# Joint last-key products, a tanh gate and a freer weight split in a capped-attention and gated-MLP kernel

## The chip, the cores and the metric

The kernel runs on one core of a Trainium2 chip. The metric is the device time of one execution in microseconds (us), as the median of several runs. The profile comes from one further execution, and its times are counted from the first instruction on the core.

## The reference

There are 4 batches, 12 heads, 448 positions and a head dimension of 64. Attention with capped scores feeds a gated MLP whose gate comes from a convolution over positions. Everything is float32 except the MLP weights, which are float64.

```python
scores = np.matmul(q, k.transpose(0, 1, 3, 2)) / np.sqrt(64)
scores = cap * np.tanh(scores / cap)
attn = np.exp(scores - max); attn = attn / (attn.sum(-1) + 1e-09)
x = np.matmul(attn, v)                     # heads joined: [4, 448, 768]
h = np.maximum(x @ w_in, 0.0)              # [4, 448, 1024]
conv_out = sum over 3 taps of conv_w[k] * h shifted by k-1 positions
gate = 1.0 / (1.0 + np.exp(-conv_out))
out = h * gate @ w_out                     # [4, 448, 768]
```

## The kernel before

**Attention.** The unit of work is a pair of heads of one batch: 24 pairs, 6 to a batch. Keys stand on the partitions and queries on the 448 free elements. A head has 448 keys, so a pair has three units `u = 0, 1, 2` of 128 keys per head (`NU = 3`) and a last unit `u = NU` with the remaining 64 keys of both heads, 128 rows in all. `scores` makes the score product of a unit into PSUM, then tanh and exp on ScalarE (L454, L458). A full unit is two products of 64 contraction rows by 128 keys, one per head, that sit in the two row halves of the array (planner mode `row`) and fill a two-bank tile `sp`. The last unit is one product of 128 by 128 (mode `full`), whose key block the host pads with zeros, into a one-bank tile `spr` from the pool `m` that the MLP uses too. Pairs 0 to 11 (`RAW`) multiply float32 directly; pairs 12 to 23 split q and k into a high and a low fp32r part (L402, L405, L256) and add three products. Two units of such pairs go into one task (`TWO = 12`).

`values` multiplies exp(scores) by V: four units, each two products of 128 by 64, one per head in a column half of the array (mode `col`), into the accumulator `acc`; the V block of the last unit is padded with zeros. All eight products of a pair are one task (`BUNDLE`).

**Key sums.** Pairs 0 to 3 (`normalize_early`) sum the keys by products with ones, eight of 128 by 32 per pair (mode `quad`). Later pairs first add the units on VectorE into `P` (L489), and the last unit by two additions on 64 partitions (L494, L497). Pairs 4 to 11 (`normalize`) sum `P` of two pairs by four products (L517) and take reciprocals of a small gathered copy that travels by DMA through DRAM (`cs`, `r_d`, `rb`). Pairs 12 to 23 (`normalize_one`, from `DIRECT = 12`) sum by two products of 128 by 64 (L631) and take the reciprocal of a whole 128x448 tile (L636). `split` then writes x as a high and a low part.

**MLP.** `feed_forward` runs 288 product steps of 128 by 128 by 448 per batch: 144 into `hps` (L674) and 144 into `ops` (L757). Between them ScalarE makes relu (L682) and the middle tap (L692), VectorE the outer taps (L700), ScalarE the sigmoid (L709) and VectorE the product with h (L715).

**Weights.** `weight_unit` turns float64 words into two fp32r parts: ScalarE scales the high word (L322), VectorE masks and shifts (L324, L326, L329), either engine makes the rounded part, VectorE the remainder. There are 12 units of 128x512 for w_in and 24 of 128x256 for w_out, which go back to DRAM (`wo`) and are loaded again in every batch.

**Order.** `Plan` orders all tasks of all engines at build time, and each engine then works through its list in that order. Of the tasks that can start, an engine's next is that of the earliest due time, from `STEP`, `FIRST` and `DUE`; TensorE adds `HOLD` for a change between `full` and a tiled mode and `CROSS` for one between tiled modes. `either` leaves the engine, ScalarE or VectorE, to the planner. All loads are issued on SP's queue. Pools bound what can be in flight: two `sp` tiles, two `acc` banks (key sums use them too), two `m` banks, 15 `e` buffers, two each for k and q.

Of the kernel before, what the change touches and what calls it, by code (L numbers as in the profile page):

```python
# [172 lines left out]
def capped_attention_gated_mlp_kernel(  # L173
# [17 lines left out]
    KW = KF + 128  # L191
# [71 lines left out]


# [42 lines left out]
    def weight_unit(src, n, due, stage, take, uses, deps, dst=None):  # L307
# [67 lines left out]
    prep, b_in, t_v, b_v = {}, {}, {}, {}  # L375
# [5 lines left out]
    def prepare(p):  # L381
# [5 lines left out]
        lk = dma("sp", 128 * KW * 4, lambda: new(p, raw_p, "kr", [128, KW]), lambda: k[b, j], ld, (), [bk],  # L387
# [3 lines left out]
        t_v[p] = dma("sp", 128 * KW * 4, lambda: new(p, raw_p, "vr", [128, KW], bufs=BUFS["v"]), lambda: v[b, j], ld + 3, (),  # L391
                     [b_v[p]], after=t0 - AHEAD["v"])
        if p in RAW:
            prep[p], b_in[p] = [lk, lq], [bq, bk]
            return
# [12 lines left out]
        def k_hi(eng):  # L408
            copy(eng, new(p, raw_p, "ks", [128, 2, KW], F32R, bufs=BUFS["s"])[:, 0], T[p]["kr"])

        def k_lo():
            sub(T[p]["ks"][:, 1], T[p]["kr"], f32(T[p]["ks"][:, 0]))
# [3 lines left out]
        c = either(KW, k_hi, due + 0.1, [lk, a], uses=[bk, bs])  # L416
        c2 = task("dve", dve(KW), k_lo, due + 0.4, [c], uses=[bk, bs])
        prep[p], b_in[p] = [a, a2, c, c2], [bs]

    def scores(units, due):  # L420

        rest = units[0][1] == NU
        n = 1 if rest else 2
        out = [{} for _ in units]
        bufs = [Buf("m" if rest else "sp") for _ in units]

        def qk():
            for (p, u), sp in zip(units, out):
                if rest:
                    sp[0] = ps_m.tile([128, 512], F32, tag="m", name="spr").rearrange("p (a s) -> p a s", a=1)  # L430
                else:
                    sp[0] = ps_s.tile([128, 2, 512], F32, tag="sp", name="sp")
                X = T[p]
                if p in RAW:
                    parts = [(X["kr"], X["qr"])]
                else:
                    parts = [(X["ks"][:, w], X["qs"][:, l]) for w, l in ((0, 0), (0, 1), (1, 0))]
                for i, (w, x) in enumerate(parts):
                    for h in range(n):
                        r = slice(0, 128) if rest else half[h]  # L440
                        nc.tensor.matmul(out=sp[0][:, h, 0:S], lhsT=w[r, 128 * u:128 * u + 128], rhs=x[r],  # L441
                                         start=i == 0, stop=i == len(parts) - 1)

        cost = sum(2 * HALF if p in RAW else 3 * PASS for p, u in units)
        t_qk = task("pe", cost, qk, due, [t for p, u in units for t in prep[p]], bufs,
                    [b for p, u in units for b in b_in[p]], mode="full" if rest else "row")
        for (p, u), sp, bsp in zip(units, out, bufs):
            t_u = when(p, u / (NU + 1))
            raw = p in RAW
            b_e[p, u] = Buf("e")  # L450

            def tanh(sp=sp, raw=raw):
                x = sp[0][:, 0:n, 0:S]
                nc.scalar.activation(out=x, in_=x, func=ACTF.Tanh, **({"scale": tsc_sb[:, 0:1]} if raw else {}))  # L454

            def exp(p=p, u=u, sp=sp):
                E[p, u] = e_p.tile([128, 2, S], F32, tag="e", name="E")
                nc.scalar.activation(out=E[p, u][:, 0:n], in_=sp[0][:, 0:n, 0:S], func=ACTF.Exp, scale=cap_sb[:, 0:1])  # L458

            t = task("act", act(n * S, True, ptr=raw), tanh, t_u + 1, [t_qk, t_tsc], uses=[bsp])  # L460
            t_exp[p, u] = task("act", act(n * S, True, ptr=True), exp, t_u + 2, [t], [b_e[p, u]], [bsp], table="exp")

    def values(p):

        b_acc[p] = Buf("acc")

        def av(us):
            if us[0] == 0:
                T[p]["acc"] = ps_a.tile([128, 512], F32, tag="acc", name="acc")
            for u in us:  # L470
                for h in range(2):
                    c = 128 * u + 64 * h
                    nc.tensor.matmul(out=T[p]["acc"][half[h], 0:S], lhsT=T[p]["vr"][:, c:c + 64],  # L473
                                     rhs=E[p, u][:, 0 if u == NU else h, :], start=u == 0, stop=u == NU)

        for us in ([range(NU + 1)] if p >= BUNDLE else [[u] for u in range(NU + 1)]):
            t_av[p] = task("pe", 2 * HALF * len(us), lambda us=us: av(us), when(p, us[-1] / (NU + 1)) + DUE["av"],
                           [t_exp[p, u] for u in us] + [t_v[p]] + ([t_av[p]] if us[0] else []), [] if us[0] else [b_acc[p]],
                           ([b_acc[p]] if us[0] else []) + [b_v[p]] + [b_e[p, u] for u in us], mode="col")
# [3 lines left out]

# [7 lines left out]
        def add_rest(h):  # L491
            P = T[p]["P"][half[h], h]
            if p >= DIRECT:
                nc.vector.scalar_tensor_tensor(out=P, in0=E[p, NU][half[h], 0], scalar=eps_key[half[h]], in1=P,  # L494
                                               op0=ALU.add, op1=ALU.add)
            else:
                nc.vector.tensor_tensor(out=P, in0=P, in1=E[p, NU][half[h], 0], op=ALU.add)  # L497

        t = [t_exp[p, 0]]
        for u in range(1, NU):  # L500
            t = [task("dve", dve(2 * S), lambda u=u: add(u), when(p, u / (NU + 1)) + 3.5, t + [t_exp[p, u]],
                      [b_P[p]] if u == 1 else [], [b_e[p, u]] + ([b_e[p, 0]] if u == 1 else [b_P[p]]))]
        t_P[p] = [task("dve", dve(S), lambda h=h: add_rest(h), when(p, 0.75) + 3.5 + h, t + [t_exp[p, NU], t_eps_key],
                       uses=[b_P[p], b_e[p, NU]]) for h in range(2)]
# [52 lines left out]
    def normalize_early(p):  # L557


        X = T[p]  # L560
# [3 lines left out]
        def sums():  # L564
            X["sm"] = ps_a.tile([128, 512], F32, tag="acc", name="sm")
            for j in range(2):
                for i in range(4):
                    u, h = 2 * j + i // 2, i % 2
                    w, x = ones[:, 0:32], E[p, u][:, 0 if u == NU else h]
                    if u == NU:  # L570
                        w = ones[:, 64 + 32 * h:96 + 32 * h]
                    nc.tensor.matmul(out=X["sm"][32 * i:32 * i + 32, 0:S], lhsT=w, rhs=x, start=j == 0, stop=j == 1)

        t = task("pe", 4 * HALF, sums, due + DUE["sum"], [t_exp[p, u] for u in range(NU + 1)] + [t_const], [bsm],
                 [b_e[p, u] for u in range(NU + 1)], mode="quad")
# [46 lines left out]
    def normalize_one(p):  # L622

        X = T[p]
        d = when(p + 1) + DUE["one"]
# [24 lines left out]
    def feed_forward(b):  # L650
# [10 lines left out]
        for f in range(NFC):  # L661
# [6 lines left out]
            for c in range(NCC):  # L668
# [14 lines left out]
                out=H[:, 1:S + 1], in_=hps[0][:, 0:S], func=ACTF.Relu), d - 10, t_h[-1:] + old + [t_const], uses=[bm])  # L683
# [24 lines left out]
            def sig(g=g):  # L708
                nc.scalar.activation(out=ct[g][:, 0:len(g)], in_=ct[g][:, 0:len(g)], func=ACTF.Sigmoid)  # L709

            ts = task("act", 0.05 + 0.39 * len(g), sig, d, [t_g[x] for x in g], uses=[bct[g]], table="sigmoid")
# [66 lines left out]
    units = [(p, u) for p in range(NP) for u in range(NU)]  # L778
    while units:
        n = 2 if units[0][0] >= TWO and len(units) > 1 else 1  # L780
        scores(units[:n], when(units[0][0], units[0][1] / (NU + 1)))
        units = units[n:]
    for p in range(NP):
        scores([(p, NU)], when(p, NU / (NU + 1)))
    for p in range(NP):
        values(p)
    for p in range(SUMPE):
# [12 lines left out]
def layout(inputs):  # L800
# [16 lines left out]
    kt = np.zeros((B, H // 2, 2 * D, KF + 128), k.dtype)  # L817
    kt[..., 0:KF] = heads_t(k)[..., 0:KF]

# [4 lines left out]
    for h in range(2):  # L824
        kt[:, :, h * D:h * D + D, KF + h * R:KF + h * R + R] = heads_t(k)[:, :, h * D:h * D + D, KF:]
        vt[:, :, h * R:h * R + R, KF + h * D:KF + h * D + D] = v2[:, :, h, KF:]
    return {
        "q": heads_t(q),
        "k": kt,
# [28 lines left out]
```

## Time and profile before

| | |
|---|---|
| runs | 434.56, 434.90, 435.56 us; median 434.9 |
| span of the profiled execution, first to last instruction | 432.9 us |
| TensorE (PE) busy | 418.6 us, 97% |
| its weight loads (PEld) | 288.1 us, 67% |
| VectorE (DVE) busy | 309.9 us, 72% |
| ScalarE (ACT) busy | 289.1 us, 67% |
| DMA queue, share of 16 engines | 49.8% |
| granted TensorE clock | 0.9 or more of full speed in each of 40 slices |

No time of the profiled execution is recorded beside its span; the span lies 2.0 us under the median of the runs. A product's busy time on PE overlaps the next one's, so the cost of a product is read from start to start of a sequence, or from the pieces of the chain that ended last, which do not overlap. A float32 product is recorded as two instructions, an fp32r one as one.

### The profile page before, as it was taken

The numbers are of one execution on the slowest core, as the hardware profiler recorded it, in microseconds if no ns is written. First come the engines' busy times: TensorE is split into PE (matmuls) and PEld (weight loads), VectorE is DVE, ScalarE is ACT, GpSimd is POOL, SyncE is SP. The second block draws the span as 40 slices with busy tenths as digits, with TensorE's granted clock in tenths as the row PEclk, the third lists the DMA queues.
The fourth block names the chain that finished last, engine by engine and source line by source line (L and its number), as shares of the span: only waits on it lengthen the run. The fifth ranks groups of instructions, "written<-read, shape, count | busy, mean of one in ns | idle before, by whom it ended". The sixth has DMA issues, their size and how long they took to land.

```text
span 432.9 us, 5890 instructions
## 1 busy us (share of the span) xinstructions
PE 418.6 (97%) x2106; PEld 288.1 (67%) x2106; DVE 309.9 (72%) x548; ACT 289.1 (67%) x412; POOL 0.2 (0%) x4
## 2 busy tenths in 40 slices
PE   7987889999999999999999999999999999999996
PEld 3222234457577676868667868668677787999995
DVE  1788899999999965589899773498899813166400
ACT  4999999988999665358888545368697811454411
POOL 0000000000000000000000000000000000000000
PEclk9999999999999999999999999999999999999999
DMA  7668557887556988650211762633000374500181
GB/s 273 217 225 263 182 181 234 274 244 254 206 161 200 345 292 263 229 210 5 70 28 44 224 225 90 202 130 120 24 2 0 131 251 148 183 0 2 30 336 53
DMA packets 37085, 70.90 MB, mean 164 GB/s; under 512 B 6336, under 2 KB 20160, under 8 KB 37056
## 3 DMA queue, kind: packets, MB, share of 16 engines
q1 hardware_dynamic: 37056, 70.53, 49.8%
q8 instruction: 17, 0.28, 0.3%
q14 instruction: 12, 0.10, 0.1%
HBM read 58.61 MB, written 11.84 MB: 163 GB/s over the span
## 4 chain that ended last, share of the span: by engine, by line
PE 78%; ACT 11%; DVE 7%; issue 2%; DMA 2%; ACTq 0%; DVEq 0%
PE ops L757 27%; PE hps L674 23%; PE acc L473 12%; PE sp L441 8%; ACT E L458 4%; ACT sp L454 4%; PE sm L631 2%; PE spr L441 2%; DVE P L489 1%; PE warm L280 1%; DMA kr<-in_k_dram 1%; DVE st_o L326 1%; ACT st_i L322 1%; DVE P L497 1%; DVE st_o L329 1%
## 5 line engine op out<-in xcount | busy, mean ns | idle before, releaser
L674 PE MATMUL hps<-x,wi_h 128*128 128x448 f32 x384 | 112.2, 373 | 0.0
L674 PEld LDWEIGHTS hps<-x,wi_h 128*128 128x128 f32 x384 | 70.8, 188 | 15.5 <-issue 6.7
L473 PE MATMUL acc<-E,vr 128*64 128x448 f32 x384 | 77.9, 546 | 0.0
L458 ACT ACTIVATE E<-sp,cap_sb 128x896 f32<-128x896 f32 x72 | 72.0, 1028 | 0.2
L674 PE MATMUL hps<-x,wi_l 128*128 128x448 f32 x192 | 70.2, 366 | 0.0
L700 DVE SCALAR_TENSOR_TENSOR ct<-hp,cw_sb,ct 128x448 f32<-128x448 f32 x64 | 43.1, 680 | 20.5 <-ACT ct L692 20.1
L473 PEld LDWEIGHTS acc<-E,vr 128*64 128x64 f32 x384 | 25.2, 136 | 44.3 <-issue 39.0
L636 DVE RECIPROCAL rb<-sm 128x448 f32<-128x448 f32 x12 | 35.5, 2956 | 16.4 <-PE sm L631 16.3
L757 PE MATMUL ops<-gh,wh 128*128 128x448 f32 x192 | 46.6, 372 | 0.3 <-ACT E L458 0.3
L757 PE MATMUL ops<-gh,wl 128*128 128x448 f32 x192 | 46.5, 367 | 0.0
L757 PE MATMUL ops<-gl,wh 128*128 128x448 f32 x192 | 43.8, 366 | 0.0
L441 PE MATMUL sp<-qr,kr 64*128 64x448 f32 x144 | 34.8, 582 | 8.7 <-ACT E L458 8.5
L253 ACT ACTIVATE osb<-ops 128x448 f32<-128x448 f32 x21 | 11.4, 544 | 46.6 <-PE ops L757 46.6
L757 PEld LDWEIGHTS ops<-gh,wh 128*128 128x128 f32 x192 | 35.3, 188 | 9.0 <-PE acc L473 1.4
L454 ACT ACTIVATE sp<-sp 128x896 f32<-128x896 f32 x36 | 31.0, 897 | 12.7 <-PE sp L441 12.6
L757 PEld LDWEIGHTS ops<-gh,wl 128*128 128x128 f32 x192 | 35.9, 188 | 4.1 <-DMA wh<-wo 0.7
L454 ACT ACTIVATE sp<-sp,tsc_sb 128x896 f32<-128x896 f32 x36 | 35.2, 1007 | 4.7 <-PE sp L441 4.7
L757 PEld LDWEIGHTS ops<-gl,wh 128*128 128x128 f32 x192 | 36.1, 188 | 3.1
L674 PEld LDWEIGHTS hps<-x,wi_l 128*128 128x128 f32 x192 | 36.1, 188 | 3.1
L441 PEld LDWEIGHTS sp<-qr,kr 64*128 64x128 f32 x144 | 11.8, 189 | 30.2 <-ACT E L458 18.1
L682 ACT ACTIVATE hp<-hps 128x448 f32<-128x448 f32 x32 | 17.4, 546 | 15.3 <-PE hps L674 13.0
L441 PE MATMUL sp<-qs,ks 64*128 64x448 f32 x216 | 26.9, 380 | 0.0
(84 smaller groups left out, 489.8 us busy)
## 6 DMA issues: line engine op xcount, KB each, us to landing
wh<-wo SPq DMA_DIRECT2D x24, 512.0 KB, 4.3
wl<-wo SPq DMA_DIRECT2D x24, 512.0 KB, 6.1
kr<-in_k_dram SPq DMA_DIRECT2D x24, 256.0 KB, 4.2
vr<-in_v_dram SPq DMA_DIRECT2D x24, 256.0 KB, 3.3
st_i<-in_moe_w_in_dram SPq DMA_DIRECT2D x12, 512.0 KB, 4.2
st_o<-in_moe_w_out_dram SPq DMA_DIRECT2D x24, 256.0 KB, 4.3
wo<-st_o SPq DMA_DIRECT2D x24, 256.0 KB, 3.6
qr<-in_q_dram SPq DMA_DIRECT2D x24, 224.0 KB, 4.3
```

The costliest lines, as they stand in the source:

```text
L253: nc.scalar.activation(out=out, in_=in_, func=ACTF.Copy)
L280: nc.tensor.matmul(out=t[:, 0:S], lhsT=ones, rhs=hp[0][:, 0:S], start=True, stop=True)
L441: nc.tensor.matmul(out=sp[0][:, h, 0:S], lhsT=w[r, 128 * u:128 * u + 128], rhs=x[r], start=i == 0, stop=i == len(parts) - 1)
L454: nc.scalar.activation(out=x, in_=x, func=ACTF.Tanh, **({"scale": tsc_sb[:, 0:1]} if raw else {}))
L458: nc.scalar.activation(out=E[p, u][:, 0:n], in_=sp[0][:, 0:n, 0:S], func=ACTF.Exp, scale=cap_sb[:, 0:1])
L473: nc.tensor.matmul(out=T[p]["acc"][half[h], 0:S], lhsT=T[p]["vr"][:, c:c + 64], rhs=E[p, u][:, 0 if u == NU else h, :], start=u == 0, stop ...
L631: nc.tensor.matmul(out=X["sm"][half[h], 0:S], lhsT=ones[:, 0:64], rhs=X["P"][:, h], start=True, stop=True)
L636: nc.vector.reciprocal(out=new(p, n_p, "rb", [128, S], bufs=BUFS["rb"]), in_=X["sm"][:, 0:S])
L674: nc.tensor.matmul(out=hps[0][:, 0:S], lhsT=w[:, c, ws], rhs=x[:, l, :], start=(c == 0 and i == 0), stop=(c == NCC - 1 and i == 2))
L682: t = task("act", act(S, True), lambda H=H, hps=hps: nc.scalar.activation(out=H[:, 1:S + 1], in_=hps[0][:, 0:S], func=ACTF.Relu), d - 10, ...
L700: nc.vector.scalar_tensor_tensor(out=ct[g][:, i], in0=H[:, o:o + S], scalar=cw_sb[:, f, o:o + 1], in1=ct[g][:, i], op0=ALU.mult, op1=ALU.add)
L757: nc.tensor.matmul(out=ops[0][:, 0:S], lhsT=W[part][:, f, :], rhs=G[l][:, f, :], start=(cnt["n"] == 0), stop=(cnt["n"] == 3 * NFC - 1))
```

## The change

1. The last keys of two pairs, r and r+1 with r even, become one joint unit. Its scores are four products of 64 by 64, row half by head and column half by pair, in float32 for all pairs (mode `sq`), into one `sp` tile; one tanh and one exp of 128x896 follow. The joint unit's values are four products of 64 by 64, row half by pair and column half by head, into the accumulators of both pairs. K and V lose their zero padding (V of odd pairs is loaded to 384 columns), and q and k stay in their buffers until the joint product.
2. The last keys enter `P` by one addition of 64x896 per pair.
3. The scaling of the weights' high word may run on either engine.
4. The relu writes h/2; the gate is tanh of the taps, and the last product (tanh + 1) * h/2.
5. `DIRECT` goes from 12 to 20, so that pairs 12 to 19 take the path of `normalize`.
6. The planner's constants change, and units are grouped by two pairs: seven units in tasks of 2, 2, 2 and 1 from pair 12 on.

```diff
-STEP = (9.5,) * 8 + (17.2,) * 16
-FIRST = 6.0
-DUE = {"w_in": (4.4, 57.93), "w_out": (63.06, 84.72), "prep": -5.0, "load": -34.0, "av": 5.0, "sum": 4.0,
-       "x": 14.0, "x0": 14.0, "one": 4.5, "rec": 2.0, "ff": 27.0, "gate": -25.0, "wq": 6.0, "wld": -15.0}
+STEP = (9.17,) * 14 + (14.59,) * 10
+FIRST = 2.12
+DUE = {"w_in": (4.4, 59.3), "w_out": (54.88, 80.43), "prep": -7.51, "load": -35.91, "av": 11.21,
+       "sum": 2.73, "x": 18.74, "x0": 15.14, "one": 3.4, "rec": 1.45, "sq": 1.88, "sq1": 4.57, "ff": 35.04,
+       "gate": -19.35, "wq": 5.98, "wld": -16.88}
-BIAS, SWITCH = {"act": 1.0, "dve": 1.0}, 0.1
-SLACK = {"pe": 0.0, "act": 0.1, "dve": 0.1, "sp": 0, "pool": 0}
-HOLD = 5.0
-CROSS = 0.0
-DIRECT = 12
+BIAS, SWITCH = {"act": 1.09, "dve": 0.78}, 0.1
+SLACK = {"pe": 0.05, "act": 0.04, "dve": 0.03, "sp": 0, "pool": 0}
+HOLD = 7.61
+CROSS = 1.11
+DIRECT = 20
...
-            x.append(task("act", n / 1200 + 0.094, lambda: nc.scalar.activation(
-                out=f32(st["A"]), in_=f32(st["H"]), func=ACTF.Abs, scale=2.0 ** -112), due, x[-1:], uses=use))
+            def rescaled(eng):
+                if eng == "dve":
+                    nc.vector.tensor_scalar(out=f32(st["A"]), in0=f32(st["H"]), scalar1=2.0 ** -112, scalar2=None,
+                                            op0=ALU.mult)
+                else:
+                    nc.scalar.activation(out=f32(st["A"]), in_=f32(st["H"]), func=ACTF.Copy, scale=2.0 ** -112)
+
+            x.append(either(n, rescaled, due, x[-1:], uses=use))
...
-                if rest:
-                    sp[0] = ps_m.tile([128, 512], F32, tag="m", name="spr").rearrange("p (a s) -> p a s", a=1)
-                else:
-                    sp[0] = ps_s.tile([128, 2, 512], F32, tag="sp", name="sp")
+                sp[0] = ps_s.tile([128, 2, 512], F32, tag="sp", name="sp")
+                if u == NU:
+                    for x in of(p, u):
+                        for h in range(2):
+                            nc.tensor.matmul(out=sp[0][half[x % 2], h, 0:S], lhsT=T[x]["kr"][half[h], KF:S],
+                                             rhs=T[x]["qr"][half[h]], start=True, stop=True)
+                    continue
...
+        def av_rest():
+            new_acc()
+            for x in (r, p):
+                for h in range(2):
+                    rows = half[x - r]
+                    nc.tensor.matmul(out=T[x]["acc"][half[h], 0:S], lhsT=T[r]["vr"][rows, KF + 64 * h:KF + 64 * h + 64],
+                                     rhs=E[r, NU][rows, h, :], start=x == p, stop=x == r)
+
+        if odd:
+            t_av[r] = task("pe", 2 * HALF, av_rest, unit_time(r, NU) + DUE["av"] + (DUE["sq"] if p < DIRECT else DUE["sq1"]), [t_exp[r, NU], t_av[r], t_v[r]],
+                           [b_acc[p]], [b_acc[r], b_v[r], b_e[r, NU]], mode="sq")
...
-        def add_rest(h):
-            P = T[p]["P"][half[h], h]
+        def add_rest():
+            P, x = T[p]["P"][rows], E[r, NU][rows]
             if p >= DIRECT:
-                nc.vector.scalar_tensor_tensor(out=P, in0=E[p, NU][half[h], 0], scalar=eps_key[half[h]], in1=P,
-                                               op0=ALU.add, op1=ALU.add)
+                nc.vector.scalar_tensor_tensor(out=P, in0=x, scalar=eps_key[rows], in1=P, op0=ALU.add, op1=ALU.add)
             else:
-                nc.vector.tensor_tensor(out=P, in0=P, in1=E[p, NU][half[h], 0], op=ALU.add)
+                nc.vector.tensor_tensor(out=P, in0=P, in1=x, op=ALU.add)
...
-                out=H[:, 1:S + 1], in_=hps[0][:, 0:S], func=ACTF.Relu), d - 10, t_h[-1:] + old + [t_const], uses=[bm])
+                out=H[:, 1:S + 1], in_=hps[0][:, 0:S], func=ACTF.Relu, scale=0.5), d - 10, t_h[-1:] + old + [t_const], uses=[bm])
...
-                nc.scalar.activation(out=ct[g][:, 0:len(g)], in_=ct[g][:, 0:len(g)], func=ACTF.Sigmoid)
+                nc.scalar.activation(out=ct[g][:, 0:len(g)], in_=ct[g][:, 0:len(g)], func=ACTF.Tanh)
...
-                t = task("dve", dve(S), lambda c=c, m=m: nc.vector.tensor_tensor(
-                    out=c(), in0=c(), in1=hp[m % len(hp)][:, 1:S + 1], op=ALU.mult), d, [ts], uses=[bct[g]])
+                t = task("dve", dve(S) + 0.06, lambda c=c, m=m: nc.vector.scalar_tensor_tensor(
+                    out=c(), in0=c(), scalar=1.0, in1=hp[m % len(hp)][:, 1:S + 1], op0=ALU.add, op1=ALU.mult), d, [ts],
+                         uses=[bct[g]])
...
-    units = [(p, u) for p in range(NP) for u in range(NU)]
-    while units:
-        n = 2 if units[0][0] >= TWO and len(units) > 1 else 1
-        scores(units[:n], when(units[0][0], units[0][1] / (NU + 1)))
-        units = units[n:]
-    for p in range(NP):
-        scores([(p, NU)], when(p, NU / (NU + 1)))
+    for r in range(0, NP, 2):
+        units = [(r, u) for u in range(NU + 1)] + [(r + 1, u) for u in range(NU)]
+        while units:
+            n = 2 if r >= TWO and len(units) > 1 else 1
+            scores(units[:n], unit_time(*units[0]))
+            units = units[n:]
```

## Rows read from the trace of the kernel before

**Rows 1.** Busy time by stretch: window, its length, then each engine (x instructions)

```profile
core 0: us, PE busy (x) PEld busy (x) DVE busy (x) ACT busy (x) POOL busy (x), PEclk, DMA share, GB/s
20.00:62.00 42.00, 34.94 (x180) 11.54 (x178) 36.52 (x72) 41.25 (x60) 0.00 (x0) 1.00 0.69 222
62.00:110.00 48.00, 46.85 (x226) 25.90 (x224) 47.51 (x115) 42.91 (x68) 0.00 (x0) 1.00 0.79 250
110.00:190.00 80.00, 80.00 (x409) 56.82 (x409) 63.87 (x123) 56.94 (x84) 0.00 (x0) 1.00 0.73 240
```

**Rows 2.** Waits of PE, whole run: total us, times, longest

```profile
PE sp L441 <- ACT E L458: 8.5, 8, 1.6
PE ops L757 <- ACT E L458: 0.3, 1, 0.3
```

**Rows 3.** Chain that ended last, the end: start, us, what

```profile
400.04 29.39 PE ops L757 x144
429.50 0.54 ACT osb L253
```

**Rows 4.** PE's timeline, attention alone: start, us, instructions

```profile
19.21 1.02 PE L441 MATMUL sp<-qr,kr 64*128 64x448 f32 x4
20.17 1.02 PE L441 MATMUL spr<-qr,kr 128*128 128x448 f32 x2
21.11 1.02 PE L441 MATMUL sp<-qr,kr 64*128 64x448 f32 x4
...
29.47 1.77 PE L441 MATMUL sp<-qr,kr 64*128 64x448 f32 x8
31.17 1.02 PE L441 MATMUL spr<-qr,kr 128*128 128x448 f32 x2
```

**Rows 5.** Chain, pieces with few or no MLP products between them

```profile
23.66 0.55 ACT st_i L322
...
34.76 3.16 PE acc L473 x16
37.91 1.64 PE sm L572 x16
...
143.10 0.76 PE spr L441 x2
...
152.84 0.89 PE sm L517 x8
```

**Rows 6.** Chain, pairs from 12 on, between MLP products

```profile
180.06 0.61 PE spr L441 x3
...
181.89 1.42 PE sp L441 x12
...
188.40 3.16 PE acc L473 x16
191.56 0.75 PE sm L631 x4
```

**Rows 7.** Groups of the whole run, shapes apart

```profile
L324 DVE TENSOR_SCALAR st_i<-st_i 128x512 uint32<-128x512 uint32 x12 | 5.1, 424 | 11.4 <-ACT st_i L322 11.3
L326 DVE SCALAR_TENSOR_TENSOR st_i<-st_i 128x512 uint32<-128x512 uint32 x12 | 8.3, 694 | 0.2
L709 ACT ACT_TABLE_LOAD x10 | 12.8, 1283 | 0.2
L636 DVE RECIPROCAL rb<-sm 128x448 f32<-128x448 f32 x12 | 35.5, 2956 | 16.4 <-PE sm L631 16.3
```

**Rows 8.** PE's timeline, the step from a tiled mode to the MLP

```profile
89.90 0.68 PE L674 MATMUL hps<-x,wi_h 128*128 128x448 f32 x2
90.42 0.37 PE L674 MATMUL hps<-x,wi_l 128*128 128x448 f32 x1
```

**Rows 9.** Groups of ACT, 20 to 62 us: busy, mean ns, idle before

```profile
L322 ACT ACTIVATE st_i<-st_i 128x512 f32<-128x512 f32 x9 | 7.1, 789 | 0.0
L458 ACT ACTIVATE E<-spr,cap_sb 128x448 f32<-128x448 f32 x5 | 3.6, 725 | 0.0
```

More of the change, by code (lines that the diff above doesn't have):

```diff
@@ L374, in capped_attention_gated_mlp_kernel @@
     E, t_exp, b_e, t_av, t_P, b_P, b_acc = ({} for _ in range(7))
-    prep, b_in, t_v, b_v = {}, {}, {}, {}
+    prep, b_in, t_v, b_v, plain, b_plain, t_rest = ({} for _ in range(7))
     def new(p, pool, tag, shape, dtype=F32, **kw):
@@ L438, in qk @@
                 for i, (w, x) in enumerate(parts):
-                    for h in range(n):
-                        r = slice(0, 128) if rest else half[h]
-                        nc.tensor.matmul(out=sp[0][:, h, 0:S], lhsT=w[r, 128 * u:128 * u + 128], rhs=x[r],
+                    for h in range(2):
+                        nc.tensor.matmul(out=sp[0][:, h, 0:S], lhsT=w[half[h], 128 * u:128 * u + 128], rhs=x[half[h]],
                                          start=i == 0, stop=i == len(parts) - 1)
-        cost = sum(2 * HALF if p in RAW else 3 * PASS for p, u in units)
-        t_qk = task("pe", cost, qk, due, [t for p, u in units for t in prep[p]], bufs,
-                    [b for p, u in units for b in b_in[p]], mode="full" if rest else "row")
+        cost = sum(2 * HALF if p in RAW or u == NU else 3 * PASS for p, u in units)
+        modes = {"sq" if u == NU else "row" for p, u in units}
+        deps = [t for p, u in units for x in of(p, u) for t in (plain if u == NU else prep)[x]]
+        uses = [b for p, u in units for x in of(p, u) for b in (b_plain if u == NU else b_in)[x]]
+        t_qk = task("pe", cost + 0.19 * (len(modes) - 1), qk, due, deps, bufs, uses, mode=modes.pop())
         for (p, u), sp, bsp in zip(units, out, bufs):
-            t_u = when(p, u / (NU + 1))
-            raw = p in RAW
+            t_u = unit_time(p, u)
+            raw = p in RAW or u == NU
             b_e[p, u] = Buf("e")
             def tanh(sp=sp, raw=raw):
-                x = sp[0][:, 0:n, 0:S]
+                x = sp[0][:, :, 0:S]
                 nc.scalar.activation(out=x, in_=x, func=ACTF.Tanh, **({"scale": tsc_sb[:, 0:1]} if raw else {}))
@@ L457, in exp, with new_acc @@
                 E[p, u] = e_p.tile([128, 2, S], F32, tag="e", name="E")
-                nc.scalar.activation(out=E[p, u][:, 0:n], in_=sp[0][:, 0:n, 0:S], func=ACTF.Exp, scale=cap_sb[:, 0:1])
-            t = task("act", act(n * S, True, ptr=raw), tanh, t_u + 1, [t_qk, t_tsc], uses=[bsp])
-            t_exp[p, u] = task("act", act(n * S, True, ptr=True), exp, t_u + 2, [t], [b_e[p, u]], [bsp], table="exp")
+                nc.scalar.activation(out=E[p, u], in_=sp[0][:, :, 0:S], func=ACTF.Exp, scale=cap_sb[:, 0:1])
+            t = task("act", act(2 * S, True, ptr=raw), tanh, t_u + 1, [t_qk, t_tsc], uses=[bsp])
+            t_exp[p, u] = task("act", act(2 * S, True, ptr=True), exp, t_u + 2, [t], [b_e[p, u]], [bsp], table="exp")
     def values(p):
+        odd, r = p % 2 == 1, p - p % 2
         b_acc[p] = Buf("acc")
+        def new_acc():
+            T[p]["acc"] = ps_a.tile([128, 512], F32, tag="acc", name="acc")
         def av(us):
-            if us[0] == 0:
-                T[p]["acc"] = ps_a.tile([128, 512], F32, tag="acc", name="acc")
+            if us[0] == 0 and not odd:
+                new_acc()
             for u in us:
@@ L472, in av, with sums_of @@
                     c = 128 * u + 64 * h
[L473 to L479, printed above, removed]
+                    nc.tensor.matmul(out=T[p]["acc"][half[h], 0:S], lhsT=T[p]["vr"][:, c:c + 64], rhs=E[p, u][:, h, :],
+                                     start=u == 0 and not odd, stop=u == NU - 1 and odd)
+        def av_rest():
+            new_acc()
+            for x in (r, p):
+                for h in range(2):
+                    rows = half[x - r]
[4 more added lines that the diff above has]
+                           [b_acc[p]], [b_acc[r], b_v[r], b_e[r, NU]], mode="sq")
+            t_rest[r] = t_av[p] = t_av[r]
+        for us in ([range(NU)] if p >= BUNDLE else [[u] for u in range(NU)]):
+            first = us[0] == 0 and not odd
+            t_av[p] = task("pe", 2 * HALF * len(us), lambda us=us: av(us), unit_time(p, us[-1]) + DUE["av"],
+                           [t_exp[p, u] for u in us] + [t_v[p]] + ([] if first else [t_av[p]]), [b_acc[p]] if first else [],
+                           ([] if first else [b_acc[p]]) + [b_v[p]] + [b_e[p, u] for u in us], mode="col")
+    def sums_of(p):
         if p < SUMPE:
             return
+        r, rows = p - p % 2, half[p % 2]
         b_P[p] = Buf("e")
@@ L557, in normalize_early @@
     def normalize_early(p):
-        X = T[p]
+        X, r0 = T[p], p - p % 2
+        parts = [(p, u) for u in range(NU)] + [(r0, NU)]
         due = when(p + 1)
@@ L568, in sums @@
                     u, h = 2 * j + i // 2, i % 2
-                    w, x = ones[:, 0:32], E[p, u][:, 0 if u == NU else h]
+                    w, x = ones[:, 0:32], E[p if u < NU else r0, u][:, h]
                     if u == NU:
-                        w = ones[:, 64 + 32 * h:96 + 32 * h]
+                        w = ones[:, 64 + 32 * (p - r0):96 + 32 * (p - r0)]
                     nc.tensor.matmul(out=X["sm"][32 * i:32 * i + 32, 0:S], lhsT=w, rhs=x, start=j == 0, stop=j == 1)
-        t = task("pe", 4 * HALF, sums, due + DUE["sum"], [t_exp[p, u] for u in range(NU + 1)] + [t_const], [bsm],
-                 [b_e[p, u] for u in range(NU + 1)], mode="quad")
+        t = task("pe", 4 * HALF, sums, due + DUE["sum"], [t_exp[x] for x in parts] + [t_const], [bsm],
+                 [b_e[x] for x in parts], mode="quad")
         t = either(S, lambda eng: copy(eng, new(p, n_p, "su", [128, S]), X["sm"][:, 0:S]), due + DUE["sum"] + 0.5, [t], [bsu],
@@ L624, in normalize_one @@
         X = T[p]
-        d = when(p + 1) + DUE["one"]
+        d = unit_time(p - p % 2, NU) + 5.0 if p % 2 == 0 else when(p + 1) + DUE["one"]
         bsm, br, bxu = Buf("acc"), Buf("rb"), Buf("xu")
@@ L706, in feed_forward, with half_tanh @@
                 continue
-            def sig(g=g):
-                nc.scalar.activation(out=ct[g][:, 0:len(g)], in_=ct[g][:, 0:len(g)], func=ACTF.Sigmoid)
-            ts = task("act", 0.05 + 0.39 * len(g), sig, d, [t_g[x] for x in g], uses=[bct[g]], table="sigmoid")
+            def half_tanh(g=g):
+                nc.scalar.activation(out=ct[g][:, 0:len(g)], in_=ct[g][:, 0:len(g)], func=ACTF.Tanh)
+            ts = task("act", 0.05 + 0.39 * len(g), half_tanh, d, [t_g[x] for x in g], uses=[bct[g]])
             for i, f2 in enumerate(g):
@@ L777, in capped_attention_gated_mlp_kernel @@
         prepare(p)
[L778 to L784 removed]
+    for r in range(0, NP, 2):
[4 more added lines that the diff above has]
+            units = units[n:]
     for p in range(NP):
         values(p)
+    for p in range(NP):
+        sums_of(p)
     for p in range(SUMPE):
@@ L823, in layout @@
         B, H // 2, 128, KF)
-    for h in range(2):
-        kt[:, :, h * D:h * D + D, KF + h * R:KF + h * R + R] = heads_t(k)[:, :, h * D:h * D + D, KF:]
-        vt[:, :, h * R:h * R + R, KF + h * D:KF + h * D + D] = v2[:, :, h, KF:]
+    for i in range(2):
+        vt[:, 0::2, i * R:i * R + R, KF:] = v2[:, i::2, :, KF:].transpose(0, 1, 3, 2, 4).reshape(B, H // 4, R, 2 * D)
     return {
         "q": heads_t(q),
-        "k": kt,
+        "k": heads_t(k),
         "v": vt,
```

38 lines of the change are left out of this document (21 added, 17 removed).

## The prediction

> **What bounds the kernel now.** The first page gives PE 97% busy and every other engine far less, but that is a mean, so I split the span into stretches. The reader is to see in [rows 1] that the bound changes. From 20 to 62 us ScalarE is busy 41.25 of 42.00 us and PE 34.94; from 62 to 110 us VectorE is busy 47.51 of 48.00; from 110 us PE is busy without a gap while the two others have a fifth to a third of their time free. The view of waits says what this costs PE: 8.5 us in eight waits for an exp that has to free an `sp` tile, all before 110 us, and 0.3 us later on [rows 2]. So the head (the first 110 us) holds PE back by 8.5 us, and the rest is set by PE's own list. The chain that ended last closes with 144 MLP steps in 29.39 us, 0.204 us each, and one eviction at 429.50 us [rows 3]. The 1152 MLP steps then take 235 us of the 432.9; the other 198 us are attention, changes of mode, the 8.5 us, and start and end. The change cuts into these 198 us, so I sum over PE's list first and ask afterwards whether the head follows.
>
> **Prices of the modes.** Two row units one behind the other take 1.70 us from start to start (29.47 to 31.17), one alone 0.96 (19.21 to 20.17) and a last unit alone 0.94 [rows 4]: 0.75 for two products side by side, or for one float32 product of 128 by 128, and 0.2 for the change of mode.
>
> The trace has no group of four 64x64 products. Its nearest row has four tiles of 128x32 side by side: two such groups take 1.64 us and one takes 0.89 [rows 5], so a group adds 0.75, the price of one product. Below 0.75 a group can't go, since one product takes as long; the other end is two at a time, as the row and column halves run today, 1.50. I take 0.75: the nearest row has four different moving operands too.
>
> The Trainium skill, page "TensorE: Matmul & The Clock Gate", section "Measured speedup vs the span model", speaks against this: four row tiles gave 3.07 times and not 4. By it a group would take 4 x 0.75 / 3.07 = 0.98 us, an estimate from the page, and 24 groups 5.5 us more than in my sum. The four column tiles of [rows 5] show no such loss; row and column halves at once no row shows.
>
> **The change, part by part**
>
> *Scores of the last keys, pairs 0 to 11.* Seven of twelve products lie between other tiled work at 0.95, five inside MLP work, where they need no change of mode, at 0.76 [rows 4, 5]: 10.45 us. Six groups at 0.75 + 0.20 are 5.70. **-4.75 us**, with groups at 1.50 about 0.
>
> *Scores, pairs 12 to 23.* Two pairs take 3 x 1.42 + 2 x 0.61 = 5.48 us [rows 6]. Afterwards two tasks of two units (2.84), one of a unit and the group (0.20 + 0.61 + 0.20 + 0.75 = 1.76) and a single unit (0.81) make 5.41. Six times 0.07: **-0.4**. The last keys gain nothing here, since three fp32r passes cost less than a float32 group and the new mode needs its own changes.
>
> *Values.* A pair takes 3.16 us for eight products [rows 6]: four times 0.75 and 0.16. Two pairs go from 6.32 to 2 x (2.25 + 0.16) + 0.95 = 5.77; twelve times 0.55: **-6.6**.
>
> *Key sums.* Pairs 12 to 19 have eight sums of 0.75 [rows 6]; the other path has four of 0.89 [rows 5]: **-2.4**. Eight reciprocals of 2.96 us leave VectorE [rows 7], which PE never waited for. In their place come 24 issues on SP's queue and a trip through DRAM; pairs 4 to 11 travel like this already, and after 110 us PE waited for nothing but 0.3 us [rows 2]: MLP steps of the batch before cover it. Without the cover PE would stand for one trip, a few us per batch.
>
> *More visits.* Behind a tiled task the first two MLP steps take 0.52 us (89.90 to 90.42) [rows 8] against 0.41. From pair 12 on, two pairs leave the MLP for three score tasks and two value runs; afterwards for four, three, and perhaps a sum: up to three more visits, 6 x 3 x 0.11 = 2.0. Some will lie side by side: **+1.0**, range 0 to 2.
>
> *Tiled modes held together.* `CROSS` lets PE stay in a tiled mode for a task due up to 1.1 us later. Each change avoided is worth 0.2; one per two pairs among the first twelve: **-1.2**, range 0 to -2.4.
>
> *Scaling, joint tanh and exp, head.* From 20 to 62 us ScalarE scales nine st_i tiles [rows 9], each a piece of 0.55 us in the chain [rows 5], and two smaller ones: some 5.7 us. On VectorE one of 512 elements costs between 0.42 (the mask, which has one source too) and 0.69 (the shifts) [rows 7]; I take 0.42. With half of them moved and 0.14 us less per pair for the joint tanh and exp, ScalarE falls from 41.25 to 37.6 us and VectorE rises from 36.52 to 38.8: the stretch could shrink from 42 to 39 us. PE sheds 0.75 us per pair there, 3.2 in all. So the head shortens by what PE sheds, its wait stays near 7 us: **0**. If the scalings stayed on ScalarE, 2.5 us of this would be lost.
>
> *Nothing on PE's path.* Ten table loads of 1.28 us for the sigmoid [rows 7] go, and those back to exp; tanh and exp alternate today without one. They lie where MLP products keep PE busy; with that cover gone the ten and as many back would be worth up to 26 us. The multiply gets a scalar, some 0.07 us on VectorE, which has time (63.87 of 80 us [rows 1]). The single addition of 64x896 and the narrower key split relieve VectorE. K and q buffers are held until the joint product, so on SP's queue the next pairs' loads, and what is queued behind them, go later; PE waited for no load today [rows 2].
>
> **Sum.** -4.75 - 0.4 - 6.6 - 2.4 + 1.0 - 1.2 = -14.35. On the span of 432.9 us that leaves 418.5; with the 2.0 us between span and median, **420.5 us**.
>
> **Rivals.** *The head does not follow.* Today the last unit's tile lies in pool `m`; it gives ScalarE some 1.0 us of work (exp alone is 0.73 busy [rows 9]) while PE is 4.80 us in values and sums (34.76 to 39.55 [rows 5]). Afterwards all seven units share two `sp` tiles, for which PE waits already [rows 2]. If ScalarE runs dry 1.0 us per pair, seven pairs give 7 us back: 427.5. Against it: the value run is split, so ScalarE's gap is shorter.
>
> *The head gains more.* If ScalarE's relief frees the `sp` tiles early enough, most of the 8.5 us of waiting goes: 412 to 413. Against it: VectorE would then be the limit, as it nearly is from 62 us on [rows 1].
>
> *Four tiles overlap in part.* A group at 1.0 us, a third of the way between the two ends, adds 24 x 0.25 = 6.0: 426.5. The rule above leads here too.
>
> *The other side: four run as two and two.* 24 x 0.75 = 18 us: 438.5, slower than before. It decides from 0.75 + 14.35 / 24 = 1.35 us per group on. For it: both halves in use at once is what no row shows. Against it: [rows 5].
>
> **Chances.** 0.2% of this kernel is 0.9 us, about what a measurement can tell. The forecast, 414 to 424: 0.52. Head does not follow, 424 to 431: 0.18. Head gains more, 409 to 414: 0.14. Partial overlap: 0.07. Two and two: 0.07, slower. Parts that cancel, within 0.2%: 0.02. So faster 0.91, same 0.02, slower 0.07. The range is 410 to 431: it leaves out the slow side, the case of no change, and the far ends of both head cases.
>
> **What would show it.** The chain should still run on PE without gaps from some 100 us on. A 64x64 group should take 0.95 us from start to start alone, six units of values and a group about 5.8 us per two pairs, and four key sums of 0.9 us replace eight. There should be one table load. The waits of PE for exp should be near 8 us, all in the head. The prediction is wrong if a group takes over 1 us, if PE waits more than 12 us in the head, or if waits for a DMA or a bank appear on PE after it.

## The result, and the profile after

The changed kernel takes 414.37 us (413.15 to 414.89 in 4 runs) against 434.73 us; the ratio is 0.9527, with a 95% interval from 0.9506 to 0.9549. The forecast was 420.5 us, within 410 to 431: the direction and the range hold, and 6 us of gain were not foreseen. The profiled execution took 414.8 us around a span of 413.0 us. Medians from here on leave out one disturbed run each of experiments 7 (441.2 us) and 12 (1003 us).

The waits of PE in the changed kernel come first (total us, times, longest), then the stretches of [rows 1].

```profile
PE sp L458 <- ACT E L477: 3.2, 5, 1.4
PE warm L286 <- DVE hp L280: 1.8, 1, 1.8
PE hps L712 <- DVE x L257: 0.6, 1, 0.6
PE sp L448 <- ACT E L477: 0.2, 1, 0.2
```

```profile
20.00:62.00 42.00, 39.78 (x226) 13.19 (x228) 40.41 (x84) 39.48 (x52) 0.00 (x0) 1.00 0.81 250
62.00:110.00 48.00, 47.68 (x250) 23.77 (x242) 47.21 (x108) 46.05 (x72) 0.00 (x0) 1.00 0.73 224
110.00:190.00 80.00, 79.75 (x444) 58.35 (x443) 63.76 (x126) 55.99 (x83) 0.00 (x0) 1.00 0.72 236
```

Without the warm-up (`warm`, the products that run before the first scores), PE waits 4.0 us in all, where it waited 8.8 us [rows 2]. This gives the split that the rest of the document uses. Call the span less these waits *PE's list*: its products, its changes of mode, and start and end. What a lower granted clock costs is in the list too. The list went from 432.9 - 8.8 = 424.1 to 413.0 - 4.0 = 409.0 us, that is -15.1 (forecast -14.35), and the waits fell by 4.8 (forecast 0). Between 20 and 62 us ScalarE is no longer full (39.48 against 41.25 us [rows 1]) and PE is busy 39.78 us instead of 34.94.

The chain that ended last shows the new prices (start, us, what); dots stand for rows of other work that are left out.

```profile
128.03 0.89 PE sm L554 x8
...
134.62 0.81 PE sp L458 x6
135.43 0.91 PE sp L448 x8
...
141.84 1.43 PE sp L458 x12
143.27 2.41 PE acc L496 x12
145.67 0.91 PE acc L504 x8
146.59 0.80 PE sp L458 x6
...
300.08 0.75 PE sm L669 x4
...
350.70 29.37 PE hps L712 x144
380.07 29.39 PE ops L796 x144
```

A group of four 64x64 products takes 0.91 us with its change of mode, in the scores (L448) as in the values (L504). Three units of values take 2.41. The last MLP steps cost what they cost in [rows 3].

Two rows of PE's timeline in the changed kernel, one of the kernel before, and four groups of the whole run of the changed kernel (busy, mean ns, idle before) show the rest:

```profile
35.51 1.89 PE L504 MATMUL acc<-E,vr 64*64 64x448 f32 x8
...
38.28 0.47 PE L712 MATMUL hps<-x,wi_h 128*128 128x448 f32 x1
```

```profile
68.66 0.92 PE L674 MATMUL hps<-x,wi_h 128*128 128x448 f32 x2
```

```profile
L330 DVE TENSOR_SCALAR st_i<-st_i 128x512 f32<-128x512 f32 x9 | 3.8, 422 | 5.9 <-DMA st_i<-in_moe_w_in_dram 5.9
L333 ACT ACTIVATE st_i<-st_i 128x512 f32<-128x512 f32 x3 | 2.1, 706 | 0.0
L674 DVE RECIPROCAL rb<-sm 128x448 f32<-128x448 f32 x4 | 11.8, 2956 | 3.5 <-PE sm L669 3.5
L290 ACT ACT_TABLE_LOAD x1 | 1.3, 1283 | 0.7 <-PEq L883 0.7
```

Nine of twelve scalings of w_in went to VectorE, at 0.42 us each as taken from [rows 7]; one table load is left. And the MLP starts at 38.28 us, thirty us before its first step in the old kernel (68.66 us). The prediction had nothing on this. The group at 35.51 us is the one of the 24 that is far off its price: the next product starts 1.82 us later, at 37.33. Its second two products start only at 36.43 us, right behind the copy of ScalarE that releases them and ends at 36.38. The view of waits does not show this wait.

### The profile page after: what moved, and what is told of

It reads as the page before. It is cut to its first block, busy times and chain, and to the rows that moved or that the text cites. A ratio compares the mean times of both kernels' runs of the same rounds, so it can differ in the third digit from the quotient of the medians.

```text
span 413.0 us, 5974 instructions
## 1 busy us (share of the span) xinstructions
PE 403.5 (98%) x2142; PEld 273.6 (66%) x2142; DVE 280.6 (68%) x525; ACT 266.4 (65%) x384; POOL 0.2 (0%) x4
## 4 chain that ended last, share of the span: by engine, by line
PE 76%; DVE 13%; DMA 4%; ACT 3%; issue 2%; SPq 1%; DVEq 0%; ACTq 0%
PE ops L796 29%; PE hps L712 27%; PE acc L496 8%; PE sp L458 7%; DVE P L527 2%; DMA st_i<-in_moe_w_in_dram 2%; PE sp L448 2%; ACT sp L473 2%; DMA st_o<-in_moe_w_out_dram 1%; PE acc L504 1%; DVE st_i L338 1%; ACT E L477 1%; PE warm L286 1%; PE sm L554 1%; DVE st_i L341 1%
## 5 line engine op out<-in xcount | busy, mean ns | idle before, releaser
L477 ACT ACTIVATE E<-sp,cap_sb 128x896 f32<-128x896 f32 x84 | 82.4, 1012 | 0.4
L496 PE MATMUL acc<-E,vr 128*64 128x448 f32 x288 | 59.8, 548 | 0.0
L473 ACT ACTIVATE sp<-sp,tsc_sb 128x896 f32<-128x896 f32 x48 | 46.4, 984 | 5.7 <-PE sp L458 4.6
L796 PE MATMUL ops<-gh,wl 128*128 128x448 f32 x192 | 45.4, 366 | 0.0
L496 PEld LDWEIGHTS acc<-E,vr 128*64 128x64 f32 x288 | 18.5, 136 | 35.9 <-issue 33.0
L527 DVE TENSOR_TENSOR P<-P,E 128x896 f32<-128x896 f32 x20 | 21.7, 1086 | 16.5 <-ACT E L477 16.4
L458 PE MATMUL sp<-qs,ks 64*128 64x448 f32 x216 | 28.5, 386 | 0.0
```

What stands on the lines that cost most here:

```text
L458: nc.tensor.matmul(out=sp[0][:, h, 0:S], lhsT=w[half[h], 128 * u:128 * u + 128], rhs=x[half[h]], start=i == 0, stop=i == len(parts) - 1)
L477: nc.scalar.activation(out=E[p, u], in_=sp[0][:, :, 0:S], func=ACTF.Exp, scale=cap_sb[:, 0:1])
L527: nc.vector.tensor_tensor(out=T[p]["P"], in0=E[p, 0] if u == 1 else T[p]["P"], in1=E[p, u], op=ALU.add)
L796: nc.tensor.matmul(out=ops[0][:, 0:S], lhsT=W[part][:, f, :], rhs=G[l][:, f, :], start=(cnt["n"] == 0), stop=(cnt["n"] == 3 * NFC - 1))
```

## The experiments

All were timed in three or more rounds beside the kernel before. "Changed" is the kernel of the diff, 414.4 us. The theories: the shorter list explains most of the gain; the waits fell because ScalarE lost scalings (A), because the MLP starts earlier (B), or because the order changed with the constants (C).

**1. Scalings on ScalarE alone.** In the changed kernel:

```diff
-            x.append(either(n, rescaled, due, x[-1:], uses=use))
+            x.append(task("act", n / 1200 + 0.094, lambda: rescaled("act"), due, x[-1:], uses=use))
```

> The changed kernel with every scaling of the weights on ScalarE again (as a Copy with a scale). PE's waits fell from 8.8 us before to 4.0 us after, and 4.9 us of the 20 us come from there. If they fell because ScalarE lost scalings, PE waits some 8 us again and the time is 418 to 419 us. If they fell because MLP steps now start at 38 us and fill the gaps, or by the planner's constants, it stays within 1 us of 414.4 us.

420.71 us, ratio 0.9682 [0.9657, 0.9707]. PE's waits:

```profile
PE sp L458 <- ACT E L477: 7.6, 6, 2.1
PE warm L286 <- DVE hp L280: 1.8, 1, 1.8
PE ops L796 <- DMA wh<-wo: 1.3, 1, 1.3
```

8.9 us, 7.6 of them for exp, as A says, although the MLP still starts at 41 us. The time is 1.7 us above A's 419, and the span is 418.9: the list grew too, by 1.0 us, of which the last section tells.

**2. The MLP held until 68 us.** In the changed kernel, for batch 0 (its first step then came at 71.10 us):

```diff
-                                [] if c else [bm], ([bm] if c else []) + b_x[b * NPB + c]))
+                                [] if c else [bm], ([bm] if c else []) + b_x[b * NPB + c], after=0.0 if b else 68.0))
```

> The changed kernel, in which the planner lets no MLP step of batch 0 start before 68 us (before, the first came at 68.66 us; in the changed kernel 17 come earlier, 3.5 us of work). If these early steps fill the head's gaps, PE's waits grow by about 3 us and the time is 417 to 418 us. If ScalarE's relief or the planner's constants made the waits shorter, the steps only move, and it stays within 1 us of 414.4 us.

423.55 us, ratio 0.9740 [0.9710, 0.9770]; more than either theory gave. (By the changed kernel's timeline 18 steps come before 68 us, not 17.) The waits are 9.3 us:

```profile
PE sp L458 <- ACT E L477: 8.1, 7, 2.2
PE warm L286 <- DVE hp L280: 1.8, 1, 1.8
PE sp L448 <- ACT E L477: 0.8, 1, 0.8
PE hps L712 <- DVE x L257: 0.4, 1, 0.4
```

So B holds as well: with the scalings moved and the constants new, the waits are back if the MLP comes late.

**3. The sigmoid again.** In the changed kernel, relu without the half, sigmoid, plain product; 20 table loads.

```diff
-                nc.scalar.activation(out=ct[g][:, 0:len(g)], in_=ct[g][:, 0:len(g)], func=ACTF.Tanh)
+                nc.scalar.activation(out=ct[g][:, 0:len(g)], in_=ct[g][:, 0:len(g)], func=ACTF.Sigmoid)
```

> The changed kernel with the sigmoid and its plain product back, so with some 20 table loads of 1.28 us on ScalarE. If MLP products hide ScalarE's loads, as forecast, the time stays within 1 us of 414.4 us. If the loads hold back exp where PE has little else to do, it rises by 2 to 5 us.

417.21 us, ratio 0.9600 [0.9579, 0.9621], 2.8 us more: the loads are not all hidden. PE's waits from 110 to 190 us, where the changed kernel has almost none:

```profile
PE sp L448 <- ACT E L477: 1.1, 1, 1.1
PE ops L795 <- DVE qs L416: 0.9, 1, 0.9
PE ops L795 <- ACT hp L720: 0.6, 1, 0.6
```

**4. Joint last keys alone, with the new constants.** The changed kernel with the old scaling (Abs, on ScalarE), the sigmoid, and `DIRECT = 14`, so that six of the eight moved pairs sum directly again; pairs 12 and 13 keep the new path.

```diff
-DIRECT = 20
+DIRECT = 14
```

> The changed kernel with only the joint last keys and the new constants: scaling by Abs on ScalarE, the sigmoid, and the direct key sums from pair 14 on (pairs 14 to 19 go back, six of the eight). If PE's list is the cause, key sums give back some 2.5 to 3 us and the rest nothing: 417 to 417.5 us. If ScalarE's relief is behind the head, 421 to 422 us.

423.43 us, ratio 0.9748 [0.9706, 0.9790]; waits 7.5 us. Both theories gave less. Neither counts the sigmoid's loads, which cost 2.8 us by themselves in experiment 3.

**5. A bank of pool m booked for the joint unit**, from product to exp, in the planner alone:

```diff
+        bm = [Buf("m") for p, u in units if u == NU]
-        t_qk = task("pe", cost + 0.19 * (len(modes) - 1), qk, due, deps, bufs, uses, mode=modes.pop())
+        t_qk = task("pe", cost + 0.19 * (len(modes) - 1), qk, due, deps, bufs + bm, uses, mode=modes.pop())
...
-            t_exp[p, u] = task("act", act(2 * S, True, ptr=True), exp, t_u + 2, [t], [b_e[p, u]], [bsp], table="exp")
+            t_exp[p, u] = task("act", act(2 * S, True, ptr=True), exp, t_u + 2, [t], [b_e[p, u]], [bsp] + (bm if u == NU else []), table="exp")
```

> The changed kernel, in which the planner books one of the two m banks for each joint unit from its product to its exp, without using it. Before, the last unit's tile lay in that pool, banks are given in the order of due times, and the first MLP step came at 68.66 us; after, it comes at 38.28 us. If the pool was what held the MLP back, its first step moves to some 60 us and the time is 420 to 424 us, as with the late MLP (423.6). If the constants or an earlier x let it start, little moves: within 1.5 us of 414.4 us.

432.44 us, ratio 0.9951 [0.9925, 0.9978]: nearly the whole gain is gone, more than either theory gave. The first MLP step is at 70.65 us, so the pool is what held the MLP back. The time is not the price of the late start alone, which is 9.2 us in experiment 2: the bank is booked in every batch, the waits are 14.0 us, of which 3.5 are for a weight tile between 110 and 190 us, and the granted clock falls twice (last section).

```profile
PE sp L458 <- ACT E L478: 8.9, 8, 2.1
PE ops L797 <- DMA wh<-wo: 3.5, 1, 3.5
```

```profile
70.65 0.67 PE L713 MATMUL hps<-x,wi_h 128*128 128x448 f32 x2
```

**6. The old kernel with the last unit's tile in `sp`.**

```diff
-        bufs = [Buf("m" if rest else "sp") for _ in units]
+        bufs = [Buf("sp") for _ in units]
...
-                    sp[0] = ps_m.tile([128, 512], F32, tag="m", name="spr").rearrange("p (a s) -> p a s", a=1)
+                    sp[0] = ps_s.tile([128, 2, 512], F32, tag="sp", name="sp")
```

> The kernel before with one thing changed: the last unit's tile is taken from the two sp tiles and no longer from m. If the pool held the MLP back, MLP steps come long before 68 us, PE's waits fall from 8.8 us by 3 us or more, and the time is 429 to 432 us. If ScalarE needs the third tile, as in the rival of the prediction, it runs dry about 1 us per pair and the time is 438 to 442 us.

436.25 us, ratio 1.0039 [1.0025, 1.0052], between the two expectations. MLP steps come early, the first at 42.30 us, but the waits grow to 10.3 us:

```profile
PE sp L441 <- ACT E L458: 10.3, 12, 1.6
```

```profile
42.30 0.92 PE L674 MATMUL hps<-x,wi_h 128*128 128x448 f32 x2
```

The free pool alone does not lower the waits. Eight units per two pairs now pass through two `sp` tiles, and all 10.3 us are waits for these tiles: this fits the rival *The head does not follow*, at a fraction of its price. That the early steps gain something and the tiles lose more is likely but not shown apart.

**7. The changed kernel with the old constants** (the two new due times kept).

```diff
-STEP = (9.17,) * 14 + (14.59,) * 10
-FIRST = 2.12
+STEP = (9.5,) * 8 + (17.2,) * 16
+FIRST = 6.0
...
-HOLD = 7.61
-CROSS = 1.11
+HOLD = 5.0
+CROSS = 0.0
```

> The changed kernel with the constants of before (steps, due times, hold, slack, bias), the two new due times kept. If the order matters little, within 2 us of 414.4 us. If the early MLP steps and the short waits come from the constants, the waits are 8 us or more again and the time is 420 us or more.

436.81 us, ratio 1.0054 [1.0022, 1.0087]; all else in the change then gives nothing. PE waits 17.3 us, now for MLP operands too:

```profile
PE sp L457 <- ACT E L476: 8.4, 7, 2.1
PE hps L711 <- ACT x L253: 2.6, 3, 1.7
PE hps L711 <- ACT hp L719: 2.5, 1, 2.5
PE ops L795 <- DMA wh<-wo: 2.2, 1, 2.2
PE warm L285 <- DVE hp L279: 1.8, 1, 1.8
PE hps L711 <- DVE x L256: 1.0, 4, 0.5
PE sp L447 <- ACT E L476: 0.6, 1, 0.6
```

Its span is 432.1, so the list is 414.8 us: still 9.3 under that of before.

**8. The old kernel with the three other parts**: scaling on either engine, tanh gate, `DIRECT = 20`.

```diff
-DIRECT = 12
+DIRECT = 20
```

> The kernel before with the three other parts alone: the scaling on either engine, the tanh gate, and the key sums of pairs 12 to 19 by the other path. Undone together in the changed kernel (six of the eight pairs) they cost 9.1 us, so if they add up, 425 to 426 us. If they only pay once the joint unit has left the pool m and shortened PE's list, the key sums alone remain: 431 to 433 us.

434.22 us, ratio 0.9996 [0.9977, 1.0016]: nothing, and neither of the two expectations. The span is 433.1 us and the waits are 10.7 us: the list is 1.7 us shorter and the waits are 1.9 us longer. MLP products now wait too:

```profile
PE sp L447 <- ACT E L464: 8.2, 7, 1.8
PE ops L764 <- ACT E L464: 1.4, 1, 1.4
PE ops L764 <- ACT osb L253: 0.6, 1, 0.6
PE hps L680 <- ACT hp L688: 0.5, 1, 0.5
```

**9. The old kernel with the new constants.** The edit of experiment 7 the other way round, in the old kernel.

> The kernel before with the constants of the changed kernel. The changed kernel with the old constants took 437.0 us. If a set of constants is good only for the kernel that it was found for, this run is slower than before too: 438 to 450 us. If the new constants are better by themselves, 426 to 432 us.

434.50 us, ratio 1.0005 [0.9987, 1.0024]. Neither of the two expectations: the new order is as good for the old kernel as its own (span 434.0, waits 9.2), and no better. The first MLP step comes at 83.98 us.

**10. Every group of joint scores made twice.**

```diff
-                    for x in of(p, u):
+                    for x in of(p, u) * 2:
                         for h in range(2):
                             nc.tensor.matmul(out=sp[0][half[x % 2], h, 0:S], lhsT=T[x]["kr"][half[h], KF:S],
```

> The changed kernel with each of the twelve groups of joint score products made twice in a row, with the same result. The planner's costs are not told. If a group of four costs 0.75 us, as the mode prices say, PE's list grows by 9.0 us: 421 to 424 us, less what falls into waits. If four products run as two and two, 1.5 us each: 430 to 433 us.

422.43 us, ratio 0.9712 [0.9694, 0.9729]: 8.1 us more. A pair of groups in the chain, to be set beside 0.91 above:

```profile
138.52 1.67 PE sp L448 x16
```

The second group costs 1.67 - 0.91 = 0.76 us: four products for the price of one. Twelve groups are 9.1 us, and the list grew by 9.2 (span 420.6, waits 2.4), as the lower price of the expectation says.

**11. No direct key sums.** `DIRECT = 24` in the changed kernel.

```diff
-DIRECT = 20
+DIRECT = 24
```

> The changed kernel with no direct key sums at all: pairs 20 to 23 take the other path too, which nobody has run. On PE's list four sums of some 0.8 us become two of 0.9 us: 413 us if only the list counts. If the trip through DRAM comes too late for the last batch or the order suffers, 416 us or more.

412.60 us (412.05 to 413.16), ratio 0.9489 [0.9471, 0.9507]: the fastest of all, 1.8 us under the changed kernel. The two intervals just touch and the runs are from two occasions, so the step is likely but not settled. Span 411.1, waits 3.2: the list is 1.1 us shorter, and no wait for the trip through DRAM shows.

**12. Direct key sums from pair 14.** `DIRECT = 14` in the changed kernel.

> The changed kernel with direct key sums from pair 14 on, so that six of the eight moved pairs go back. By the list six sums of 0.75 us replace three of 0.89: 416 to 417 us. If the reciprocals of 2.96 us on VectorE hold something back, or the order suffers, 418 us or more.

415.93 us, ratio 0.9568 [0.9551, 0.9584]: 1.6 us more, where the list says 1.8. No profile of it is read.

The profiled executions side by side (us; list is span less PE's waits without the warm-up):

| kernel | span | PE's waits | PE's list | median of runs |
|---|---|---|---|---|
| before | 432.9 | 8.8 | 424.1 | 434.7 |
| changed | 413.0 | 4.0 | 409.0 | 414.4 |
| 1 scalings on ScalarE | 418.9 | 8.9 | 410.0 | 420.7 |
| 2 late MLP | 419.6 | 9.3 | 410.3 | 423.6 |
| 3 sigmoid | 416.2 | 5.6 | 410.6 | 417.2 |
| 4 joint last keys alone | 420.1 | 7.5 | 412.6 | 423.4 |
| 5 bank of m booked | 426.7 | 14.0 | 412.7 | 432.4 |
| 6 old, tile in sp | 434.4 | 10.3 | 424.1 | 436.3 |
| 7 changed, old constants | 432.1 | 17.3 | 414.8 | 436.8 |
| 8 old, three parts | 433.1 | 10.7 | 422.4 | 434.2 |
| 9 old, new constants | 434.0 | 9.2 | 424.8 | 434.5 |
| 10 groups twice | 420.6 | 2.4 | 418.2 | 422.4 |
| 11 no direct sums | 411.1 | 3.2 | 407.9 | 412.6 |

Where a median lies far above its span (2, 4, 5, 7), the runs of that kernel spread. In 2, 5 and 7 the longer runs tend to have the lower mean granted clock: in 7 the profiled run took 433.9 us at 0.996, and others took 439.8 and 439.9 us at 0.984. So part of these medians is clock that the profiled execution does not show. In 4 the clock does not explain the spread.

## Why the prediction was right, and where it fell short

**PE's list was sized well, in part by luck.** -15.1 us came where -14.35 were summed. A group with its change of mode was put at 0.95 and took 0.91. Two pairs' values were put at 5.77 and take 2 x 2.41 + 0.91 = 5.73. The scores of two late pairs were put at 5.41: two tasks of 1.43, one of 0.81 and 0.91, one of 0.81 make 5.39. Six key sums moved were worth 6 x 0.75 - 3 x 0.89 = 1.8 us, and experiment 12 gives 1.6. So the prices hold, but the terms do not all: added up by kind over PE's timeline, from start to start and without waits, the scores fell by 5.3 us (put at 5.15), the values by 5.0 (6.6), the key sums by 3.4 (2.4), and the MLP products by 1.4, where *More visits* had put +1.0. PE does not leave the MLP more often but less: the MLP products lie in 27 stretches, where the kernel before has 43. These errors nearly cancel. The -1.2 for modes held together has no rows of its own.

**The bounds of the 64x64 group are settled at the lower end.** Experiment 10 measures 0.76 us. The rivals of two and two (1.50) and of a partial overlap (1.0) fall. The page "TensorE: Matmul & The Clock Gate" of the Trainium skill, section "Measured speedup vs the span model", would have led to 0.98 us, an estimate by its 3.07 for four row tiles. With 448 columns of float32 in two row and two column halves the runs show 0.76, nearly a full four, and the measurement decides.

**The step that failed is the term for the head.** It read: the head shortens by what PE sheds, "its wait stays near 7 us: **0**". It measured -4.8 us, towards the rival in which the head gains more, to which 0.14 had gone; the sign that the waits for exp would be near 8 us failed, with 3.4. That rival named ScalarE's relief alone. The argument against it, that VectorE would be the limit, did not hold: from 62 to 110 us VectorE is busy 47.21 of 48.00 us, and PE 47.68. The engine balance in that step was near enough: from 20 to 62 us ScalarE was put at 37.6 and VectorE at 38.8 us, and 39.48 and 40.41 were found. But the step let a wait go only if the head became shorter. It overlooked that PE can have other work in it: with the last unit out of pool m, the planner may give m's banks to the MLP, and its first step moves from 68.66 to 38.28 us. Experiments 2 and 5 show that this is needed, and experiment 1 that the scalings on VectorE are needed too, since the waits come back to 8.9 us or more with any one undone. Experiments 6, 8 and 9 show that none of the causes tried in the old kernel (free pool, relief of ScalarE, new order) lowers its waits by itself. How the 4.8 us would divide has therefore no answer in shares. Whether the free pool, the relief and the new order together would do it without the joint unit was not tried.

**"Nothing on PE's path" was half wrong.** The table loads were costed at nothing, covered by MLP products. In the changed kernel they are worth 2.8 us (experiment 3): PE waits 1.6 us more, and its list is 1.6 longer. In the old kernel, scaling, gate and key sums together gave nothing (experiment 8), as they would if the cover held there; but that run does not separate the three. That the cover became thin when PE's list grew shorter is not shown.

**The constants were costed too low.** The prediction gave them -1.2 us, for tiled modes held together. Without them the changed kernel is no faster than the old one (experiment 7): 5.8 us of list and 13.3 us of waits. Of the list 5.1 us are MLP products, in 43 stretches again instead of 27 (245.7 against 240.7 us); the forecast had nothing on this, and which constant does it was not tried. That 436.8 us is the time of a kernel in an order that suits another; it does not say that the new values are better as such, and experiment 9 says they are not: there the MLP lies in 30 stretches and takes 1.1 us less than before, but the attention products take 2.0 us more. What the joint unit alone would give in an order of its own stays open.

**The rival "the head does not follow" did not come**, though its mechanism is real: in experiment 6, where all last units pass through the two `sp` tiles and nothing relieves ScalarE, the waits rise by 1.5 us and not by 7.

## What to carry to other kernels

Split the span into the bounding engine's list and its waits, and price an edit in each by itself: the list came out of modes and counts to within a microsecond here, though not term by term; the waits did not. Ask of each buffer that a change frees what else was queued for that pool; here a PSUM bank let the MLP start thirty us earlier. A kernel whose order is fixed at build time has to be ordered anew with each edit before the edit is judged: with the old order this change of 20 us looks like nothing (experiment 7).

## What the hardware showed unexpectedly

In experiments 1 and 2 the list grew by 1.0 and 1.3 us without one more product. PE's timeline of experiment 1 shows a wait of 2.11 us, and the products right behind it are slower (start, us, instructions, wait before):

```profile
31.12 2.55 PE L458 MATMUL sp<-qr,kr 64*128 64x448 f32 x8 [2.11 <-ACT E L477]
33.59 2.73 PE L610 MATMUL sm<-E,ones 128*32 128x448 f32 x16
36.25 2.48 PE L496 MATMUL acc<-E,vr 128*64 128x448 f32 x12
```

```profile
32.00:38.00 6.00, 6.00 (x32) 1.67 (x32) 2.27 (x5) 5.32 (x7) 0.00 (x0) 0.72 0.87 286
```

The two score units take 2.47 us to the next start instead of 1.70 [rows 4], the sixteen instructions of the key sums 2.66 instead of 1.64 [rows 5], and the mean granted clock from 32 to 38 us is 0.72 (the column behind POOL): for part of that time PE ran at 1.2 and not at 2.4 GHz. The two rows lose 1.8 us; the list grew by less, since the group that took 1.82 us in the changed kernel takes 0.91 here. In experiment 2 the clock falls to the same 0.72 in the six us around a wait of 2.2 us, while in the kernel before, with no wait over 1.6 us, and in the changed one, with none over 1.4, it stays at 1.00 there. The lists of experiments 4 and 8 hold one such stretch each, experiment 7 one behind a wait of 2.45 us at 93.11 us, and experiment 5 two, the second behind the 3.48 us for the weight tile; the other profiled kernels have none while PE still has products. So a wait can cost PE more than its own length. But not every such wait does: in experiment 7 the clock stays at 1.00 around one of 2.11 us in the head, while in experiment 8 it is 0.78 from 20 to 26 us, with a wait of 1.79 us there. For experiment 7 a row of PE's timeline, and the six us around it:

```profile
33.49 1.02 PE L457 MATMUL sp<-qr,kr 64*128 64x448 f32 x4 [2.11 <-ACT E L476]
32.00:38.00 6.00, 4.51 (x28) 1.49 (x32) 5.04 (x11) 4.70 (x6) 0.00 (x0) 1.00 0.73 209
```

What decides between them these runs do not show.
